# A written-out instruction order searched anew behind a common beginning: engines and PSUM banks of a long-convolution and MLP kernel

## The chip, the cores and the metric

The kernel runs on one core of one Trainium2 chip. The time is the device time of one execution in microseconds; a smaller one is better. The core has five engines that matter here, each with an instruction queue of its own that is worked off strictly in order: TensorE (PE, matmuls and weight loads, the latter shown as PEld), ScalarE (ACT), VectorE (DVE), GpSimd (POOL) and SyncE (SP, which issues nearly all DMAs). Engines wait for one another through semaphores. Matmul results land in PSUM, which has eight banks of 512 float32 values per partition; ACT or DVE must copy a result out ("evacuate" it) before PE may write that bank again.

## The reference

Two blocks, A and B, are applied twice to x of shape 1 x 2048 x 512, with the same k, v and weights each time:

```
def _A_ref(q, k, v, shift_k, ssm_k, ssm_D):
    ...                                   # k_shift: a causal filter of 4 taps along the sequence
    kv = k_shift * v
    ...
    y_f = kv_f * kf_f[None, :, :, :]      # FFT of kv times FFT of the 2048-tap filter ssm_k
    y = irfft2(y_f) ...                   # first 2048 positions, as bfloat16
    y = y + kv * ssm_D[None, None, :]
    return q * y
def _B_ref(x, w1, b1, w2, b2):
    y = _layernorm(x, axis=-1)
    h = _gelu(jnp.einsum("bsd,df->bsf", y, w1) + b1)          # 512 -> 1376
    return jnp.einsum("bsf,fd->bsd", h, w2) + b2              # 1376 -> 512
x = x + _A_ref(_layernorm(x), A_k, A_v, A_shift_k, A_ssm_k, A_ssm_D)
x = x + _B_ref(_layernorm(x), ...)
```

The last two lines stand twice. The convolution's y depends on k, v and the filter alone, so it is computed once and used in both layers.

## The kernel before, in words

**Two stages.** The first (up to about 83 us) computes y for all 2048 positions by a Fourier transform made of matmuls. The second runs two layers of norm, multiply by y, add, norm, and the MLP; in it all weights lie in SBUF.

**The first stage.** The 512 channels are worked in groups of 4 (128 groups). The steps, with the tags that the texts use: *ht*, the filter transposed (L528); *h1* and *h2*, the filter's two transform stages (L545, L558; 16 tiles each); *fir*, the four-tap filter of k and its product with v, on PE for channels 0 to 255 (L589, L606, L613) and on DVE for channels 256 to 511 (twelve products and sums of 128 x 2048 by L450 and two that multiply by v); *x1*, the first transform stage of kv (L545, 16 tiles); *x2*, its second stage (L651, 16 tiles), and behind each tile a product with the filter's transform on DVE (L450, 128 x 2048); *i1* and *i2*, the inverse transform's two stages (L674, 16 tiles; L731, 10 tiles). From x2 on the channels come in two parts, 0 to 255 and 256 to 511 (tags x2_0 and x2_64, and so on). Each tile of h1, h2, x1, x2 and i1 fills two PSUM banks, so four of them can be open at a time, and each is evacuated by one instruction of L453, on ACT or on DVE. Sixteen DMAs on SP copy the filter's transform to other partitions between h2 and the products (dma(dst, src) at the end of the h2 loop).

**The second stage.** The 2048 positions are 16 slices of 128. Layer 0 takes them in blocks of 1, 1, 2, 2, 2, 2, 2, 2, 2 slices, layer 1 in four blocks of 4. For each slice DVE computes a variance (L754, L756), POOL the inverse root (L760, L762), DVE the norm (L768), the product with y and the sum (L450), then a second variance and norm. The normed slice is transposed, by PE for slices 0 and 1 of layer 0 (L814, evacuated by L453), by a DMA on SP for all others (L807). Eleven tiles of the first MLP matmul per block (tag m1, L827) are each evacuated by a gelu on ACT (L832); the second MLP matmul takes a slice in three groups of 4, 4 and 3 steps (tag m2, L860), and DVE adds the result to x (L864). The last slice of layer 1 is cut into three column ranges (L849, L853). Output DMAs go out by pairs of slices.

**What sets the order.** Nothing is scheduled at run time. The code records 1114 operations, numbered in the order of recording, with what each reads and writes. Three written-out tuples of class Prog decide the rest: ORDER lists all operations, and each engine's queue is the part of ORDER that falls to it; SECOND lists the evacuations that go to the second of their two permitted engines (ACT first, DVE second); BANKS gives the first PSUM bank of each tile. arrange() reads them, and sync() works out the waits that they need: an operation waits for all earlier ones it depends on, and the first matmul of a tile waits for the evacuation of the tile that had its banks before.

```
        for at, i in enumerate(self.ORDER):
            o = self.ops[i]
            o.eng = o.engs[i in second]
            ...
            if tl is not None and tl.base is None:
                tl.base = self.BANKS[tl.i]
                for b in range(tl.base, tl.base + tl.nb):
                    if last[b] is not None:
                        for p in [p for p in last[b].ops if p.eng != PE] or last[b].ops[-1:]:
```

Of the kernel before, what the change touches and what calls it, by code (L numbers as in the profile page):

```python
# [38 lines left out]
class Prog:  # L39
# [3 lines left out]

    G = 4
    ORDER = (
# [43 lines left out]
    SECOND = (  # L89
        63, 64, 66, 67, 69, 72, 89, 97, 105, 127, 155, 161, 169, 175, 177, 215, 221, 239, 291, 349, 392)  # L90
    BANKS = (
# [7 lines left out]


    def __init__(self, nc):
        self.nc = nc
# [798 lines left out]
```

## Time and profile before

| | |
|---|---|
| median of 3 runs | 242.38 us (241.93 to 243.59) |
| span of the profiled execution, first to last instruction | 238.8 us |
| PE busy | 226.2 us (95%), 2312 matmul records |
| DVE busy | 171.6 us (72%) |
| ACT busy | 138.3 us (58%) |
| POOL busy | 41.3 us (17%) |
| granted TensorE clock | 1.000 |

The profiled execution's span is 3.6 us shorter than the median of the three runs; what lies around the span (start and end of the launch) makes the rest. The busy share of PE is no measure of its load, since matmul records overlap: a record of 379 ns can be followed by the next one some 220 ns later. The predictions' sums therefore use distances from start to start. An operation's number below is its number in ORDER; the trace has the instructions of each engine in that order, so each one's time can be read off.

### The profile page before, as it was taken

What the parts mean: (1) busy time and instruction counts of PE and PEld (TensorE: products, weight loads), DVE (VectorE), ACT (ScalarE), POOL (GpSimd) and SP (SyncE); (2) the same over time, 40 slices, a digit from 0 to 9 for tenths busy, and PEclk for the clock granted to TensorE, in tenths of its full rate; (3) what the DMA queues carried; (4) which work ended last, traced back from release to release, by engine and by line L of the source; (5) the groups of instructions that cost most, each with busy time, mean ns of one, the idle gap of its engine ahead of it and who ended that gap; (6) DMA issues with size and microseconds to landing.
All of it is one profiled execution on the core that took longest, in us unless ns stands there. A gap on an engine that the chain in (4) does not pass through costs nothing.

```text
span 238.8 us, 5555 instructions
## 1 busy us (share of the span) xinstructions
PE 226.2 (95%) x2312; PEld 151.6 (63%) x2332; DVE 171.6 (72%) x359; ACT 138.3 (58%) x225; POOL 41.3 (17%) x77
## 2 busy tenths in 40 slices
PE   7987989886999999999999999999999999999995
PEld 3875778875899886766766667644444444444543
DVE  0979999999999999999887999693793312030035
ACT  2598799999999995642754444342782042454100
POOL 2179000000013444041230310400220200000000
PEclk9999999999999999999999999999999999999999
DMA  6999949999960003111122022240013021310024
GB/s 241 364 342 383 383 148 253 249 272 309 379 227 0 3 0 68 26 23 31 37 47 44 0 48 44 45 88 3 0 22 66 3 44 31 101 44 3 0 71 148
DMA packets 37035, 27.40 MB, mean 115 GB/s; under 512 B 19506, under 2 KB 29969, under 8 KB 37010
## 3 DMA queue, kind: packets, MB, share of 16 engines
q1 hardware_dynamic: 36446, 26.91, 37.8%
q8 instruction: 18, 0.29, 0.5%
q10 hardware_dynamic: 564, 0.14, 0.4%
q14 instruction: 7, 0.06, 0.1%
HBM read 16.82 MB, written 2.10 MB: 79 GB/s over the span
## 4 chain that ended last, share of the span: by engine, by line
PE 77%; ACT 9%; DMA 4%; DVE 4%; SPq 3%; issue 3%; ACTq 0%
PE ps L860 31%; PE ps L827 30%; ACT ar L453 9%; PE ps L674 5%; PE ps L731 3%; SPq L439 3%; PE ps L545 3%; DMA ar<-in_A_ssm_k_dram 2%; DVE ar L453 2%; DMA ar<-ar 2%; PE ps L528 1%; PE ps L606 1%; PE ps L849 1%; DVE sm L754 1%; PE ps L589 1%
## 5 line engine op out<-in xcount | busy, mean ns | idle before, releaser
L832 ACT ACTIVATE ar<-ps,sm 128x256 bf16<-128x256 f32 (+4 forms) x143 | 64.7, 525 | 72.5 <-PE ps L827 68.1
L827 PE MATMUL ps<-ar 128*128 128x256 bf16 (+4 forms) x568 | 84.2, 297 | 0.2
L860 PE MATMUL ps<-ar 128*128 128x512 bf16 (+1 forms) x329 | 79.0, 379 | 0.6
L453 ACT ACTIVATE ar<-ps 128x1024 bf16<-128x1024 f32 (+1 forms) x81 | 72.5, 1057 | 9.0 <-PE ps L511 4.5
L827 PEld LDWEIGHTS ps<-ar 128*128 128x128 bf16 (+1 forms) x572 | 52.9, 100 | 29.8 <-ACT ar L832 0.5
L450 DVE TENSOR_TENSOR ar<-ar 128x512 bf16<-128x512 bf16 (+3 forms) x106 | 63.6, 634 | 2.0 <-DMA ar<-in_A_k_dram 1.3
L860 PEld LDWEIGHTS ps<-ar 128*128 128x128 bf16 (+1 forms) x341 | 33.1, 98 | 34.3 <-ACT ar L832 0.3
L864 DVE TENSOR_TENSOR ar<-ar,ps 128x512 bf16<-128x512 bf16 x31 | 20.6, 680 | 47.3 <-PE ps L860 47.3
L754 DVE BATCH_NORM_STATS2 sm<-ar 128x6 f32<-128x512 bf16 (+1 forms) x68 | 42.8, 647 | 0.1
L768 DVE TENSOR_SCALAR ar<-ar,sm 128x512 bf16<-128x512 bf16 x64 | 25.0, 407 | 7.8 <-POOL sm L762 5.2
L760 POOL TENSOR_SCALAR sm<-sm 128x2 f32<-128x2 f32 (+2 forms) x26 | 6.0, 232 | 93.9 <-DVE sm L756 93.3
L762 POOL TENSOR_TENSOR sm<-sm 128x2 f32<-128x2 f32 (+2 forms) x26 | 21.6, 832 | 2.2
L545 PE MATMUL ps<-ar 128*64 128x128 bf16 x512 | 17.1, 221 | 1.4 <-issue 0.8
L545 PEld LDWEIGHTS ps<-ar 128*64 128x64 bf16 x512 | 14.9, 110 | 3.2 <-issue 1.0
L674 PE MATMUL ps<-ar 128*128 128x128 bf16 x256 | 15.0, 220 | 0.6 <-ACT ar L453 0.6
L674 PEld LDWEIGHTS ps<-ar 128*128 128x128 bf16 x256 | 14.7, 114 | 0.8 <-ACT ar L453 0.8
L453 DVE CAST ar<-ps 128x1024 bf16<-128x1024 f32 x11 | 13.0, 1212 | 0.3 <-PE ps L558 0.3
L651 PE MATMUL ps<-ar 128*128 128x64 bf16 x256 | 9.8, 194 | 3.2 <-ACT ar L453 2.7
L453 DVE COPY ar<-ps 128x2048 bf16<-128x2048 bf16 (+1 forms) x8 | 8.2, 1024 | 6.4 <-PE ps L528 6.3
L651 PEld LDWEIGHTS ps<-ar 128*128 128x128 bf16 x256 | 8.2, 98 | 4.7 <-ACT ar L453 3.9
L756 DVE BATCH_NORM_AGGREGATE sm<-sm 128x2 f32<-128x6 f32 (+1 forms) x64 | 9.9, 171 | 0.3
L558 PE MATMUL ps<-ar 128*128 128x128 bf16 x128 | 8.6, 220 | 0.8 <-ACT ar L453 0.8
(34 smaller groups left out, 78.1 us busy)
## 6 DMA issues: line engine op xcount, KB each, us to landing
ar<-tab_s SPq DMA_DIRECT2D x16, 256.0 KB, 9.6
ar<-ar SPq DMA_DIRECT2D x16, 256.0 KB, 4.2
ar<-in_A_ssm_k_dram SPq DMA_DIRECT2D x4, 512.0 KB, 5.3
ar<-in_A_k_dram SPq DMA_DIRECT2D x8, 256.0 KB, 7.6
ar<-in_A_v_dram SPq DMA_DIRECT2D x8, 256.0 KB, 9.6
ar<-in_A_q_dram SPq DMA_DIRECT2D x4, 512.0 KB, 7.9
out_dram<-ar SPq DMA_DIRECT2D x7, 256.0 KB, 2.1
ar<-in_B_w_dram SPq DMA_DIRECT2D x1, 1376.0 KB, 12.6
```

The source lines that it names most:

```text
L450: return P.op(eng, lambda e: e.tensor_tensor(o, a, b, op), reads=[a, b] + list(more), writes=[o])
L453: f = {ACT: lambda e: e.activation(dst, src(), AF.Copy), DVE: lambda e: e.tensor_copy(dst, src())}
L545: r = e.matmul(Q(tl, 64 * ri, 64, i * 128, [1, 128]), w, m, start=True, stop=True)
L651: r = e.matmul(Q(tl, 0, 128, i * pitch, [1, n]), w, m, start=True, stop=True)
L674: r = e.matmul(Q(tl, 0, 128, i * 128, [1, 128]), w, m, start=q == 0, stop=q == 1)
L754: P.op(DVE, lambda e, sj=sj, x=x: e.bn_stats(sj, x), reads=[x], writes=[sj])
L762: P.op(POOL, lambda e: e.tensor_tensor(r, v, hf, ALU.pow), reads=[v, hf], writes=[r])
L768: P.op(DVE, lambda e: e.tensor_scalar(o, x, m, r, ALU.subtract, ALU.mult), reads=[x, m, r], writes=[o])
L827: r = e.matmul(Q(tl, 0, rows, 0, [1, w]), a, m, start=dk == 0, stop=dk == 3)
L832: P.op(ACT, lambda e, dst=dst, tl=tl, rows=rows, bias=bias, w=w: e.activation(dst, Q(tl, 0, rows, 0, [1, w]), AF.Gelu_apprx_tanh, bias=bia ...
L860: r = e.matmul(Q(tl, 0, 128, 0, [1, 512]), ins[fc][0], ins[fc][1], start=fc == 0, stop=fc == 10)
L864: P.op(DVE, lambda e, x=x, tl=tl: e.tensor_tensor(x, x, Q(tl, 0, 128, 0, [1, 512]), ALU.add), reads=[x], writes=[x], tile=tl)
```

## The change

ORDER, SECOND and BANKS get other values; nothing else differs but one blank line. The recorded operations, their sizes and their dependencies are the same 1114. Each engine's queue keeps its beginning: PE's first 31 operations (up to the first filter matmuls of channel block 0, started at 27.6 us), ACT's first 22 (up to the second h2 evacuation, 26.2 us), DVE's first 23 (to 31.7 us), SP's first 40. Behind that the queues hold the same work in another order. Thirteen evacuations change engine: h2 127, x1 161, 175 and 177, x2 215 and i1 239 go from DVE to ACT; h2 137, x1 163, 165 and 213, x2 218, i1 249 and i2 314 go from ACT to DVE. So DVE has 20 of the L453 evacuations of the transform's and transposes' tiles where it had 19. The first lines of the change, and SECOND, which shows the engines:

```
     ORDER = (
-        49, 0, 47, 8, 7, 1, 3, 6, 48, 14, 71, 68, 5, 72, 18, 17, 15, 12, 4, 69, 9, 70, 50, 16, 65, 13, 19, 94, 2, 53, 73, 96, 51, 52, 11,
...
+        49, 8, 0, 47, 1, 7, 48, 9, 6, 3, 4, 2, 14, 5, 18, 17, 15, 71, 12, 16, 13, 72, 68, 19, 11, 50, 69, 305, 65, 51, 28, 10, 52, 70, 73,
...
     SECOND = (
-        63, 64, 66, 67, 69, 72, 89, 97, 105, 127, 155, 161, 169, 175, 177, 215, 221, 239, 291, 349, 392)
+        63, 64, 66, 67, 69, 72, 89, 97, 105, 137, 155, 163, 165, 169, 213, 218, 221, 249, 291, 314, 349, 392)
     BANKS = (
...
```

The queues that result, where they differ most (numbers of matmuls in a row on PE, from the h2 stage on):

```
before: ... x1 160, x2 64, x1 64, x2 160, i1 64, x2 32, i1 112, i2 4, i1 80, i2 52, transposes 4, i2 8, m1 4, transposes 4, m1 44, m2 4, ...
after:  ... x1 144, x2 16, x1 32, x2 32, x1 16, x2 16, x1 48, x2 144, i1 32, x2 16, i1 32, x2 32, i1 192, i2 56, transposes 4, i2 8, m1 4, transposes 4, m1 72, m2 4, ...
before, last: ... m2 20, last slice 11, m2 45, last slice 22
after, last:  ... m2 69, last slice 33
```

On DVE an evacuation (213) stands between the products of x2's first part; before, one variance of layer 0 (376) stood between those of its second part. On SP the sixteen copies of the filter's transform stand as 4, 11 and 1 with the loads of q earlier and the load of W1 last.

More of the change, by code (lines that the diff above doesn't have):

```diff
@@ L45 @@
     ORDER = (
[43 rows of a table removed]
[43 rows of a table added]
     SECOND = (
-        63, 64, 66, 67, 69, 72, 89, 97, 105, 127, 155, 161, 169, 175, 177, 215, 221, 239, 291, 349, 392)
+        63, 64, 66, 67, 69, 72, 89, 97, 105, 137, 155, 163, 165, 169, 213, 218, 221, 249, 291, 314, 349, 392)
     BANKS = (
[7 rows of a table removed]
[7 rows of a table added]
     def __init__(self, nc):
```

100 rows, old and new, of tables (BANKS, ORDER) are left out of this document.

## The prediction

> **What bounds the kernel.** I read the page first: its busy line and the slices show PE at 9 from a third of the span on, DVE and ACT at 9 before that.
>
> ```profile
> PE 226.2 (95%) x2312; PEld 151.6 (63%) x2332; DVE 171.6 (72%) x359; ACT 138.3 (58%) x225; POOL 41.3 (17%) x77
> ...
> PE   7987989886999999999999999999999999999995
> PEld 3875778875899886766766667644444444444543
> DVE  0979999999999999999887999693793312030035
> ACT  2598799999999995642754444342782042454100
> ```
>
> So there are two regimes, and the windows table says where the border lies (columns: length, then busy time with instructions of PE, PEld, DVE, ACT and POOL, clock, DMA share, GB/s).
>
> ```profile
> 50.00:60.00 10.00, 7.33 (x186) 6.06 (x181) 10.00 (x10) 10.00 (x13) 0.00 (x0) 1.00 0.97 294
> 60.00:70.00 10.00, 9.45 (x179) 9.21 (x177) 10.00 (x11) 10.00 (x12) 0.52 (x1) 1.00 0.95 349
> ...
> 100.00:110.00 10.00, 9.95 (x63) 6.00 (x63) 9.96 (x29) 4.68 (x13) 3.83 (x8) 1.00 0.15 30
> ...
> 200.00:210.00 10.00, 9.95 (x48) 4.50 (x47) 1.61 (x3) 3.21 (x6) 0.00 (x0) 1.00 0.21 66
> ```
>
> Up to about 65 us ACT and DVE have no idle time and PE waits; afterwards PE has none. How full PE is there I take from the chain of work, whose pieces give the distance from matmul to matmul.
>
> ```profile
> 59.08 5.80 ACT ar L453 x6
> 64.92 6.56 PE ps L674 x112
> 71.49 0.44 PE ps L731 x4
> 71.92 4.47 PE ps L674 x80
> 76.39 5.68 PE ps L731 x52
> ...
> 83.76 2.57 PE ps L827 x44
> ...
> 203.89 4.32 PE ps L827 x20
> ...
> 224.86 9.68 PE ps L860 x44
> ```
>
> A 128-column matmul comes every 58 ns, one of 256 every 109, one of 512 every 216 (4.32/20). The first m1 matmul starts at 83.08 and the last matmul ends at 236.37, 153.3 us later. The work between: 341 of L860 and 176 of L827 at 216 ns (111.7), 308 at 109 (33.6), 88 at 57 (5.0), the last slice's 33 (2.4) and some transposes (0.3), together 153.0. **PE has no idle time worth naming after 83 us, and nothing in the change makes this work smaller.** The tail behind the last matmul is 2.4 us (one addition, one output DMA).
>
> Before 83 us PE does lose time. From 24.67 (first h2 tile) to 59.42 (first i1 tile) its groups at their own distances add up to 26.1 us in a stretch of 34.7: 8.6 us of waiting. From 59.42 to 83.08 it loses 0.8.
>
> **The change, stage by stage.** Durations are spacings in the timeline:
>
> ```profile
> 25.32 5.61 ACT L453 ACTIVATE ar<-ps 128x1024 bf16<-128x1024 f32 x6 [2.58 <-PE ps L558]
> 26.02 3.48 DVE L450 TENSOR_TENSOR ar<-ar 128x2048 bf16<-128x2048 bf16 x3
> ```
>
> Six evacuations in 5.61 us, one alone 1.02: 0.91 us each on ACT. Likewise 1.13 us for each 128 x 2048 instruction of DVE, and 1.13 for an evacuation on DVE.
>
> *To 25 us*: same queues, 0.
>
> *25 us to the first i1 tile of the second part* (before: 284 at 68.59). What ends last is the last product, since i1_64 reads all of them. DVE's queue from 173 (24.87 us) to that product holds, before, 27 of L450, four of L613, six evacuations and one variance (0.60); after, the same without the variance. Before: 42.8 us of work and 0.5 of waiting for PE (ahead of 127, at 40.20), the last product ending at 68.21. After: 42.2 of work. It waits too: evacuation 137 needs PE tile 136, fourth-last of h2; followed by hand through PE's and ACT's slots, 136 ends at 38.9 where DVE is free at 38.5, 0.5 us. Near the end product 271 is free 0.3 us ahead of ACT's evacuation 270. So 67.9 to 68.1, a gain of 0.1 to 0.3. PE reaches 292, the first i1_64 tile, when ACT has emptied the banks of 250: ACT's 49 evacuations from 121 to the last of i1_0 are as many as before, with 0.3 us of waiting in both (197 behind x1_2, which needs the DVE filter's last product). I get 292 at 68.4 against 68.59: **-0.2**, and for what my hand-followed waits may miss in some 45 alternations, -0.6 to +0.6.
>
> The copies on SP lie in this stretch. The long batch starts when h2 is done, at about 40.3 (before 41.5), and holds 11 copies where it had 9:
>
> ```profile
> 41.46 7.91 SPq L439 DMA_DIRECT2D ar<-ar x9
> ```
>
> 0.88 us each, and 4.2 (median) to landing. The four that product 231 needs are done with the eighth, 40.3 + 7.1 + 4.2 = 51.6; DVE comes there at 54.0. Product 256 needs the eleventh (54.2, DVE at 58.6), 274 the sixteenth, behind three loads (about 60, DVE at 63.1). Cover 2.4 to 4.4 us: cost 0. If it went, DVE, which has no idle time here, would pass the delay on in full. W1, now the last load, has until 83 us; before, SP's last load was issued at 59.2. The bias loads and POOL's copies of them stand earlier and wait for nothing that is late.
>
> *i1_64 to the first m1*: eight i1 tiles (0.92 each), ten i2 tiles (6.99) and four transposes (0.23) are 14.55 us of PE; before took 14.49 from 284 to 83.08, so PE alone bounds it. After: the same list, 68.4 + 14.55 = **82.95**, if nothing else comes late. What can: the norm of slice 0 (347), on which the transposes 348 wait. It follows i2 evacuation 324 (ACT, after PE tile 323 ends at 78.1, so to 78.8), then two products, two sums and a variance on DVE (with other work between, 1.3 us), 1.0 on POOL, the norm: 81.7. PE is there at 81.9. Cover 0.2 us, thin. Evacuation 314, now on DVE, waits for PE tile 313 at 76.3, with DVE ready at 75.7; all else on DVE stands behind it, and that 0.6 is in my count.
>
> *Second stage*: the same PE work, so the question is whether PE gets a wait. I set PE's running sum from 82.95 against DVE's. The late ones are the transposes of blocks 2 and 3: last norm ends at 89.6 and 92.9, SP issues two transposes of 1.3 us one behind the other, landing 2.5 after the issue: 92.2 and 95.7; PE comes at 92.9 and 96.4. Cover 0.7 each. Before had no more: block 3's second transpose was issued at 95.00 and PE took it at 97.52 without a wait. From block 4 on the cover is 1.3 to 3.5 us. DVE is 96% busy there, and I counted 3 us of waits for POOL in by 119 us; before has 4.1 from 83 to 175. Banks: of the tiles that are written again within 1.3 us of the matmul that their evacuation needs (3 for DVE's), before has 36 and after 18; the tightest stands at 0.71, and before went without a wait at 0.51. So **0**, bounded by 0 and +1.5 (both covers missed by half a microsecond or more).
>
> *Tail*: the last output goes through SP instead of ACT's queue, 32 KB landing in 1.5 or 1.6 us: 0.
>
> **Sum**: 238.8 - 0.2 = 238.6 us of span. The median lies 3.6 above the profiled span, and so I say 242.2 us against 242.38, **no change that can be told**; on this kernel about 1% (2.4 us) is what a measurement tells surely from none.
>
> A rule speaks against my floor: the Trainium skill (Perfetto Trace Analysis, Identifying the Most-Contended Engine) calls matmul busy time a bad metric and the share of LDWEIGHTS a good one. By it the PEld row, 63% here and 45% at 200 to 210 us, leaves PE room, and an order could take much more than 0.2 us. The same skill's TensorE: Matmul & The Clock Gate gives 215.7 ns from start to start for 512 columns; the trace has 216 and agrees. I hold to the spacings.
>
> **Rivals.** *Nothing moves* (0.66): as above, 241.4 to 243.2.
>
> *PE room* (0.03): PE's spacing could be shortened by better mixing of wide and narrow matmuls, hiding weight loads (98 ns) behind the wide ones. For: PEld at 45%. Against: 216 ns for 512 columns in long runs and in short ones alike (pieces of x3 and x44). If weight loads cost the 128-column ones 10 ns each, the 344 of i1 and m1 give -3.4 us: 238.8.
>
> *The front shortens by more* (0.08): i1's first tile is ready at 58.7 instead of 59.4, and if PE's 0.8 us of waiting up to 83 goes as well, -1.0 to -1.5: 241.
>
> *The thin covers fail* (0.11): the norm of slice 0 or the transposes of blocks 2 and 3 come late by half a microsecond each: +0.5 to +1.5, 243.4.
>
> *Slower, by one mechanism* (0.12): DVE falls behind between 41 and 66 us because ACT and DVE alternate as suppliers of PE. In the after queue x1_0's 163 and 165 are on DVE between filter products, and x2 cannot start before 165 (44.9). If PE's tiles reach DVE 0.6 us late at each of the five evacuations that it has there, the last product ends 3 us later, and as PE is full from there on, all of it is in the time: 245.2. It decides from the point where DVE idles at all between 41 and 66 us; before did not.
>
> That the change has no effect because PE's work is fixed is the first case. Chances: faster by over 1%: 0.03; within 1%: 0.85; slower by over 1%: 0.12. The range takes in the front's gain and the thin covers, and up to part of the last rival: 241.0 to 244.4.
>
> **What the profile after will show.** Last x2 product ending at 67.9 to 68.1; first i1_64 matmul near 68.4; first m1 near 83.0; then PE pieces that add up to 153.3 without a wait over 0.2 us; span 238.6. Wrong if DVE shows idle time between 41 and 66 us, if PE waits on DVE or a DMA before L814 or L827, or if W1 lands after 83 us.

## The result, and the profile after

The changed kernel takes **244.82 us** (median of 8 executions, 243.09 to 247.13), the kernel before, run beside it, 241.7 us. The ratio is 1.0111, with a 95% interval of 1.0083 to 1.0139: **slower by about 1.1%**. That lies above the forecast of 242.2 us and above its range. (The ratios in this document compare fast executions alone, of the changed kernel seven of the eight, so they needn't equal the quotient of the medians.)

In every execution the time is the span and 1.8 us (245.71 and 243.9 in the profiled one). The profiled execution of before, with its span of 238.8, was therefore one of about 240.6, below all eight that were timed (the lowest is 241.25).

The page of the changed kernel: the busy line, and the slices of PE, DVE, ACT and the granted clock. Line numbers are one lower than before (L826 is the first MLP matmul, L859 the second, L831 the gelu, L806 the transposes).

```profile
PE 229.0 (94%) x2313; PEld 153.8 (63%) x2332; DVE 177.3 (73%) x360; ACT 137.5 (56%) x224; POOL 41.5 (17%) x77
...
PE   7996999887899999799999999999999999999996
...
DVE  0889599999999999988997987975778652020233
ACT  2488399999999993482355182253363333347000
...
PEclk9999799999999999999999999999999999999999
```

Two slices of PE stand out: a 6 in the fourth slice (18 to 24 us) and a 7 in the seventeenth (98 to 104 us). The second one is inside the stage that I had called full. The list of PE's waits behind 84 us, of the kernel before (first fence, an empty list under its heading) and of the changed kernel in two profiled executions; the columns are the sum, the number and the longest, in us:

```profile
core 0 of [0], span 238.8 us
engine line waited for: us in total, times, longest us
```

```profile
PE ps L826 <- ACT ar L831: 1.6, 1, 1.6
PE ps L826 <- issue: 0.2, 1, 0.2
PE ps L826 <- DMA ar<-ar: 0.2, 1, 0.2
```

```profile
PE ps L826 <- DMA ar<-ar: 2.1, 1, 2.1
PE ps L826 <- ACT ar L831: 1.3, 1, 1.3
```

All of them are waits of a block's first m1 tile for its transposed slices. Where the list names the gelu on ACT, the tile waits for several semaphores, and the transpose is the last of them: in the first profile block 3's tile (operation 499) starts at 101.22, the second transpose of the block (496) landed at 101.13. Measured against the usual distances from matmul to matmul, PE waits 2.09 us behind the first m1 tile in the first profile and 3.62 in the second, where in the profile of before it waited for nothing (-0.02).

The chain of work between 84 and 150 us shows what has changed. Before, it runs over PE alone; in the changed kernel (second profile) over DVE, POOL and the transposes:

```profile
by line: PE ps L827 54.4%; PE ps L860 43.9%; ACT ar L832 1.3%; issue 0.7%
```

```profile
by line: DVE sm L753 28.7%; DVE ar L449 15.9%; DVE ar L767 13.5%; POOL sm L761 10.6%; DVE ar L863 8.0%; DMA ar<-ar 6.2%; DVE sm L755 5.7%; issue 4.1%; POOL sm L759 3.0%; ACT ar L452 2.9%; PE ps L826 1.6%; PE ps L859 0.7%; ACT ar L831 0.4%; 
...
144.57 4.09 DMA ar<-ar
148.71 1.05 PE ps L826 x8
```

The last two lines are the end of that chain: one transpose (758, block 8) that lands 4.09 us after its issue, and the m1 tile that waits for it. In the first profile the same transpose took 2.40:

```profile
146.68 2.40 DMA ar<-ar
149.12 1.05 PE ps L826 x8
```

**The front.** In the first profile the first h2 evacuation starts at 28.20 us instead of 25.32, although nothing of the queues up to there has changed. The rows of 20 to 30 us (columns as in the prediction) show a lower granted clock there, first the changed kernel, then the kernel before:

```profile
20.00:30.00 10.00, 7.39 (x94) 5.75 (x90) 7.43 (x8) 5.06 (x6) 4.50 (x4) 0.83 1.05 382
```

```profile
20.00:30.00 10.00, 8.27 (x114) 6.85 (x116) 9.67 (x9) 7.42 (x9) 3.79 (x2) 1.00 1.05 382
```

This belongs to the execution, not to the order: the second profile of the changed kernel has its first h2 evacuation at 26.10, and two of the experiments below, which have PE's front of the kernel before, have theirs at 27.16 and 27.17. From the first h2 evacuation to the first m1 tile it is 57.88 us in both profiles of the changed kernel and 57.76 before. So the stretch that I had worked out at most length takes the same time, and the loss is behind 84 us.

### The profile page after: what moved, and what is told of

Read it like the earlier page. It is cut to its first block, busy times and chain, and to the rows that moved or that the text cites. A ratio compares the mean times of both kernels' runs of the same rounds, so it can differ in the third digit from the quotient of the medians.

```text
span 243.9 us, 5564 instructions
## 1 busy us (share of the span) xinstructions
PE 229.0 (94%) x2313; PEld 153.8 (63%) x2332; DVE 177.3 (73%) x360; ACT 137.5 (56%) x224; POOL 41.5 (17%) x77
## 4 chain that ended last, share of the span: by engine, by line
PE 49%; DVE 20%; ACT 17%; POOL 8%; issue 4%; DMA 1%; POOLq 0%; DVEq 0%
PE ps L859 19%; PE ps L826 18%; ACT ar L452 17%; DVE sm L753 8%; PE ps L673 5%; DVE ar L449 4%; DVE ar L767 4%; POOL ar L519 4%; POOL sm L761 3%; PE ps L527 2%; DVE ar L863 2%; DVE sm L755 2%; PE ps L498 1%; PE ps L605 1%; PE ps L848 1%
## 5 line engine op out<-in xcount | busy, mean ns | idle before, releaser
L831 ACT ACTIVATE ar<-ps,sm 128x256 bf16<-128x256 f32 (+4 forms) x143 | 64.4, 529 | 74.3 <-PE ps L826 74.0
L826 PE MATMUL ps<-ar 128*128 128x256 bf16 (+5 forms) x568 | 82.2, 296 | 2.1 <-ACT ar L831 1.6
L859 PE MATMUL ps<-ar 128*128 128x512 bf16 (+1 forms) x330 | 77.5, 379 | 0.6
L826 PEld LDWEIGHTS ps<-ar 128*128 128x128 bf16 (+1 forms) x572 | 53.2, 100 | 30.5 <-ACT ar L831 1.8
L449 DVE TENSOR_TENSOR ar<-ar 128x512 bf16<-128x512 bf16 (+3 forms) x106 | 64.5, 635 | 1.8 <-DMA ar<-in_A_k_dram 0.6
L859 PEld LDWEIGHTS ps<-ar 128*128 128x128 bf16 (+1 forms) x341 | 33.1, 98 | 35.9 <-ACT ar L831 0.6
L753 DVE BATCH_NORM_STATS2 sm<-ar 128x6 f32<-128x512 bf16 (+1 forms) x68 | 43.4, 651 | 0.7
L767 DVE TENSOR_SCALAR ar<-ar,sm 128x512 bf16<-128x512 bf16 x64 | 24.5, 402 | 11.7 <-POOL sm L761 11.7
L673 PE MATMUL ps<-ar 128*128 128x128 bf16 x256 | 15.0, 220 | 0.9 <-DVE ar L449 0.5
L452 DVE CAST ar<-ps 128x1024 bf16<-128x1024 f32 (+1 forms) x12 | 14.0, 1171 | 0.2 <-PE ps L557 0.2
L755 DVE BATCH_NORM_AGGREGATE sm<-sm 128x2 f32<-128x6 f32 (+1 forms) x64 | 10.7, 175 | 1.0
L519 POOL TENSOR_SCALAR ar<-ar,sm 128x128 bf16<-128x128 bf16 x8 | 9.3, 1157 | 0.8
```

Of the source, the lines that this page charges most:

```text
L449: return P.op(eng, lambda e: e.tensor_tensor(o, a, b, op), reads=[a, b] + list(more), writes=[o])
L452: f = {ACT: lambda e: e.activation(dst, src(), AF.Copy), DVE: lambda e: e.tensor_copy(dst, src())}
L519: P.op(POOL, lambda e, o=o, t=t: e.tensor_scalar(o, IDN, t, None, ALU.mult), reads=[IDN, t], writes=[o])
L673: r = e.matmul(Q(tl, 0, 128, i * 128, [1, 128]), w, m, start=q == 0, stop=q == 1)
L753: P.op(DVE, lambda e, sj=sj, x=x: e.bn_stats(sj, x), reads=[x], writes=[sj])
L767: P.op(DVE, lambda e: e.tensor_scalar(o, x, m, r, ALU.subtract, ALU.mult), reads=[x, m, r], writes=[o])
```

## The experiments

Two theories. **O**: the new order of DVE's queue makes norms, and with them the transposes, late for PE. **L**: the 16 KB loads of PE's own instructions (18 in a run, DMA queue 8, kind "instruction") meet the transposes and make them land late. The rival of both: the front. In the texts written ahead of the runs, Theory 1 is O and L together and Theory 2 the front; Theory A is L and Theory B is O. Numbers are operation numbers; "waits" are PE's waits behind the first m1 tile in the profiled execution, summed from the distances in the trace as above. The texts written ahead of the runs speak of 36 and of two matmuls more; as issued they are 32 and none, and the table says so.

| kernel | waits, us | median, us | ratio to before, 95% interval |
|---|---|---|---|
| changed kernel, again | 3.62 | 244.87 | 1.0118 (1.0072 to 1.0164) |
| its front, second stage of before | 1.45 | 243.09 | 1.0068 (1.0040 to 1.0095) |
| front of before, its second stage | 4.12 | 245.36 | 1.0136 (1.0097 to 1.0175) |
| three variances later | 6.61, of which 5.06 ahead of blocks 3, 4 and 8 | 246.98 | 1.0175 (1.0121 to 1.0228) |
| changed, 32 matmuls more | 2.10 | 243.52 | 1.0092 (1.0059 to 1.0126) |
| before, unaltered (2 matmuls meant) | 0.64 | 241.23 | 0.9979 (0.9946 to 1.0011) |
| before, 32 matmuls more | -0.01 | 241.28 | 0.9996 (0.9957 to 1.0035) |
| before, taps earlier | 0.63 | 241.51 | 0.9974 (0.9940 to 1.0008) |
| changed, eight norms ahead | 1.30 | 242.58 | 1.0051 (1.0023 to 1.0079) |
| eight norms, 32 matmuls | 1.20 | 242.57 | 1.0039 (1.0005 to 1.0074) |
| eight norms, three variances | 1.63 | 242.90 | 1.0030 (1.0001 to 1.0060) |
| before, a norm made late | 1.52 | 243.24 | 1.0056 (1.0027 to 1.0085) |

The kernel before took 241.58, 241.63 and 241.85 us beside the first, second and third four of these rows.

### The changed kernel again

No edit.

> The changed kernel, unaltered, profiled a second time. In its first profile two places are late: the filter's first h2 evacuation at 28.20 us (before 25.32; the queues up to there are the same), and PE's wait of 1.75 us ahead of the first m1 tile of block 3 (operation 499), whose second transpose (496) landed at 101.13 because the first (498) took 2.33 us to issue while a 16 KB load of PE's instructions was under way at 96.12. Theory 1 (thin cover in the second stage): the wait of 1.5 to 2.1 us stands in this profile too, with the 2.3 us issue; the late h2 does not have to. Theory 2 (the loss is in the front, by what chance does at the start): the wait at block 3 is under 0.5 us here, and the time follows the first h2 evacuation. Median 244 to 245 us, ratio 1.008 to 1.014 by both.

Measured: 244.87 us. The wait at block 3 is there again (1.51 us), with the slow issue of the first transpose (2.03 us, landing 3.14 after its start), and the late h2 is not. A wait of 2.23 at block 8 comes in, which was 0.31 in the first profile. So Theory 1 holds and Theory 2 falls. The executions at full clock of the changed kernel lie in two heaps, 243.1 to 243.5 and 244.6 to 245.4; that block 8's wait, which is there or not, makes the two is likely but only argued, since two profiles show it.

### Each half alone

```
front of the changed kernel  = PE up to 391, ACT to its last i2 evacuation (318), DVE up to 392, POOL up to 389, SP up to 302
front of the kernel before   = PE up to 391, ACT to its last i2 evacuation (328), DVE up to 392, POOL up to 389, SP up to 301
behind it: all other operations in the order of the other kernel
```

> Front of the changed kernel (up to the last transposes of slice 1, the last h2-to-i2 evacuations and their DVE work), then the queues of the kernel before for the second stage. Nothing is left out. Theory 1: no wait of PE behind the first m1 tile, ratio 0.997 to 1.003. Theory 2 or a slower front order: ratio 1.007 to 1.014, as the changed kernel itself.

> The other half alone: front of the kernel before, second stage of the changed one. Theory 1: PE waits 1.5 to 2.1 us ahead of block 3's first m1 tile and 0.3 us each ahead of blocks 8 and 10, ratio 1.006 to 1.010. A slower front order as the cause: ratio 0.997 to 1.003.

Measured: 1.0068 for the changed front, against the forecast of Theory 1, and 1.0136 for the changed second stage, more than the forecast. The trace tells why the first is not 1.000: PE waits 1.0 us ahead of tile 368 in block 1 (the list names the gelu on ACT, 0.8 us), and 0.55 us ahead of block 2 (453), whose transpose had 0.27 us to spare in the kernel before. The likely reason, argued only, is the seam: the second stage of before is timed against its own front. The other half has about 1 us of such waits ahead of block 3 too, and then 0.17 (block 3), 0.76 (block 4) and 2.20 us (block 8). So the halves don't add up to the whole, but in each the excess time (1.5 and 3.8 us) is about the sum of PE's waits behind 84 us (1.45 and 4.12).

### Three variances behind block 3's second norm

```
 DVE of the changed kernel
-... 488, 581, 484, 445, 485, ... 530, 532, 497, 583, 582, 495, 538, 584 ...
+... 488, 484, 445, 485, ... 530, 532, 497, 495, 581, 583, 582, 538, 584 ...
```

> The changed kernel with three variance operations of blocks 5 (581, 583, 582; 0.69, 0.69 and 0.16 us on DVE) moved behind block 3's second norm (495), so that block 3's norms end about 0.7 and 1.4 us earlier; all else as in the changed kernel. Theory 1: the wait at 499 falls from 1.75 to between 0 and 0.95 us (0.95 if the first transpose still takes 2.3 us to issue), the time falls by 0.8 to 1.75 us: ratio 1.001 to 1.008 where the changed kernel has 1.011. Theory 2 or the front: no change, ratio 1.008 to 1.014.

Measured: 1.0175, above the changed kernel's 1.0111, though the two intervals overlap. In the profiled execution the granted clock was at half from 150.6 to 154.0 us, which makes most of the other 1.6 us of the 6.61. At its place the edit did what Theory 1 said: the wait at 499 fell from 1.51 to 0.69. But PE came earlier to the next blocks and found their transposes later: 1.98 us at block 4, 2.37 at block 8. There two transposes landed 4.17 and 4.46 us after their issue; in both a load of PE's instructions had started 1.95 us after it. This set the two theories O and L against each other.

### Moving the loads: 32 matmuls more

Each x2 tile issues its first matmul again, which writes the same values. That changes no queue's order, but PE's instruction loads come some 250 instructions apart, so all later ones move.

```
-                for i, w, m in ins:
+                for i, w, m in ins[:1] * (2 + (k0 < 32)) + ins:
```

(With `(k0 == 0)` in place of the bracket: the run meant to have two matmuls more.)

Both edits do less than the texts below say. `f` runs when the queues are written out, after the loop over `k0` has ended, and reads the last value, 112. So `k0 < 32` and `k0 == 0` are false in every tile: the first edit adds two matmuls to each of 16 tiles, 32 in all, and the second adds none. The traces agree: this line has 256 weight loads in the kernel before, 288 with the first edit and 256 with the second. **The run with two matmuls is the kernel before, unaltered, a second time.**

> The changed kernel with 36 matmuls more: in each x2 tile the first matmul is issued two times more (four of the tiles: three times more), writing the same values. That is about 2.1 us more of PE work (36 x 58 ns), in a stretch where PE waits. It moves every later 16 KB load of PE's instructions, which come every 256 instructions of PE, ahead by 72 instructions, that is 4 to 8 us. By the positions in the two profiles of the changed kernel no load then falls between the issue and the landing of a transpose of blocks 2 to 8, save one at the start of a transpose of block 6. Theory A (the loads, colliding with the transposes, make them late): PE waits under 0.5 us in all behind the first m1 tile where the changed kernel waits 2.1 and 3.6, every transpose lands within 2.4 to 2.6 us of its issue, and the time falls by 1.5 to 3.5 us although work was added: ratio 0.998 to 1.005 against the kernel before. Theory B (thin cover alone: DVE's norms come too late in the new order): waits stay at 1.5 to 3.6, time as the changed kernel or up to 2 us longer, ratio 1.010 to 1.020.

> The kernel before with the same 36 matmuls more: the control for what they cost themselves. The loads then lie clear of the transposes, save at the very start of two with covers of 2.3 and 1.4 us. Theory A: no wait in the second stage, and what is measured is the cost of the 36 in the front: 0 to 1 us, ratio 0.999 to 1.005. If 36 of them cost more than 2.4 us here, the run with the changed kernel has to be read against that.

> The kernel before with two matmuls more, one in the first x2 tile of each part (0.1 us of PE work, where it waits). It moves the later instruction loads ahead by four instructions, 0.3 to 0.5 us at blocks 2 and 4: the load near the second transpose of block 2 (446) then starts some 1.85 us after its issue and that near the second of block 4 (548) some 2.0, where it was 2.28 and 2.31. Theory A: loads that start 1.85 to 2.0 us after the issue made the landing 1.5 to 2.0 us later in three profiles, and the kernel before has covers of 0.3 and 0.05 us there, so PE gets waits of 1.2 to 2 us at block 4 and perhaps as much at block 2; ratio 1.005 to 1.014. Theory B: two matmuls in the shadow change nothing, ratio 0.998 to 1.002.

Measured, in the changed kernel: block 3's first transpose lands again as it should, and its wait is gone. The DMA view of the stretch in which it is issued, with its 16 KB load (the kernel with eight norms ahead, where this transpose is the same) and without (32 matmuls more):

```profile
q8 instruction: 1, 0.02, 6.9%
issues: line engine op xcount, KB each, median us to landing
ar<-ar SPq DMA_TRANSPOSE x1, 3.1
```

```profile
DMA packets 0, 0.00 MB, mean 0 GB/s; under 512 B 0, under 2 KB 0, under 8 KB 0
## 3 DMA queue, kind: packets, MB, share of 16 engines
issues: line engine op xcount, KB each, median us to landing
ar<-ar SPq DMA_TRANSPOSE x1, 2.4
```

The median fell from 244.8 to 243.5 although work was added, less than Theory A's forecast (0.998 to 1.005), and the intervals of the two ratios overlap. What stayed are waits behind transposes that landed within 2.4 to 2.7 us of their issue: 0.61 us at block 4, 0.34 at block 6, 0.93 at block 8, 0.37 at block 10. So L is not all of it; these are O's, but for 0.3 us of the 0.61, where the landing took 2.68 us instead of 2.4.

In the kernel before, the same 32 cost nothing (0.9996), though three transposes of blocks 6 and 8 now landed 3.6 to 4.2 us after their issue, as the loads had moved onto them. They had 1.4 to 2.3 us to spare, and 0.7 and 1.8 were left. This is the view at the issue of the first transpose of block 8 (758), before and with the 32:

```profile
ar<-ar SPq DMA_TRANSPOSE x1, 2.4
```

```profile
ar<-ar SPq DMA_TRANSPOSE x1, 4.2
```

The run with two matmuls tests neither theory, as it adds none. What it shows is how much the kernel before differs from itself: a ratio of 0.9979, whose interval takes in 1, and another place for a load. The load at block 2 stayed where it was (2.27 us behind the issue, 2.28 before), the one at block 4 came 3.7 us earlier (22.3 us behind the first m1 tile, 26.0 before), slowed the issue of that block's first transpose to 1.85 us and gave a wait of 0.66 us. The place of a load is thus not fixed to the instruction. In the run of the next section PE's queue is that of the kernel before too, and the same load came at 22.3 us, with a wait of 0.64 at block 4. What else sets it stays open.

### The start: tap matrices earlier on POOL

```
 POOL of the kernel before
-53, 67, 64, 44, 45, 56, 59, 57, 60, 310, 54, 61, 58, 55
+53, 56, 59, 67, 57, 60, 64, 44, 45, 61, 58, 54, 55, 310
```

> The kernel before with POOL's first operations in another order: the diagonal tap matrices that the first filter tile needs stand ahead of the two small additions (64, 67) and two memsets, so that they end near 17 us instead of 22.6. It tests whether the start (up to the filter's first h2 evacuation, 25.3 us before, 26.1 and 28.2 in the changed kernel's profiles) hangs on POOL. If it does: first h2 evacuation earlier by 0.3 to 1 us and the time with it, ratio 0.996 to 0.999. If PE's own chain to 154 (end 23.09) sets it: no change, ratio 0.999 to 1.001.

Measured: 0.9974, no difference that the interval tells, nor does it decide between the two forecasts; the unaltered kernel before gave 0.9979 in the last section. The trace says more. The tap matrix 58 started at 14.86 us instead of 19.96, but PE's tile 154, which stands ahead of the fir tile that needs it (172), has its second matmul at 22.27 us, 22.08 before. Tile 172 went on at 24.06 (23.15 before), at half the granted clock from 22.54 us on. So in this profile POOL doesn't set the start.

### DVE's order alone

```
 DVE of the changed kernel
-549, 686, 688, 589, 691, 547        +549, 547, 686, 688, 589, 691
-697, 472, 793, 746, 869, 698, 651, 653
+697, 651, 653, 472, 793, 746, 869, 698
-876, 817, 807, 885, 886, 804, 755, 815, 949, 950, 757
+876, 755, 757, 817, 807, 885, 886, 804, 815, 949, 950
-903, 732, 684, 955, 905, 956, 959, 968, 962, 963, 960, 901
+903, 905, 901, 732, 684, 955, 956, 959, 968, 962, 963, 960
```

> The changed kernel with eight norms of DVE moved ahead in its queue (547 of block 4 behind 549; 651 and 653 of block 6 behind 697; 755 and 757 of block 8 behind 876; 905 and 901 of block 10 behind 903); block 3, PE, ACT, POOL and SP as in the changed kernel. In the run with 36 more matmuls the transposes of these blocks landed within 2.7 us of their issue and PE still waited for them, 0.61, 0.34, 0.93 and 0.37 us (net 2.1 us), since DVE did other work ahead of the norms. Theory O (DVE's order makes the norms late, the loads of PE's instructions add to it): the waits at blocks 4, 6, 8 and 10 go, 1.5 us at block 3 stays (load behind the first transpose); the time falls by 1 to 2.3 us against the changed kernel: ratio 1.002 to 1.008. Theory L (the loads alone): moved norms meet loads as before; no change, ratio 1.008 to 1.014.

> Both together: the eight norms ahead, and the 36 repeated matmuls in the x2 tiles, which keep the loads of PE's instructions off the transposes of block 3. Theory O: no wait of PE over 0.3 us behind the first m1 tile, the whole loss is back: ratio 0.997 to 1.003. If 1.005 or more remains, something else than these waits costs time in the changed kernel, and the front would be the place.

> The eight norms ahead, and for block 3 the three variance operations (581, 583, 582) behind its second norm (495), without the 36 matmuls. The three variances alone brought block 3's wait from 1.5 to 0.7 us, but the waits at blocks 4 and 8 grew to 2.0 and 2.4, by loads that met the transposes. Theory O: with norms early enough a late landing is covered, so waits sum to 0.5 to 1.5 us, ratio 1.001 to 1.006. Theory L: 1.010 or more.

Measured: 242.58 us, ratio 1.0051; its interval ends below that of the changed kernel (1.0079 against 1.0083). **Eight moved norms, and nothing else, take the excess of the median from 3.1 to 0.7 us, that of the ratio from 1.1 to 0.5%.** The waits at blocks 4, 6, 8 and 10 are gone, the 1.4 at block 3, which the edit doesn't touch, is what is left, and the chain of 84 to 150 us runs over PE again (the ACT in both views is that wait, whose transpose landed last):

```profile
PE ps L827 <- ACT ar L832: 1.3, 1, 1.3
```

```profile
by line: PE ps L827 53.3%; PE ps L860 44.5%; ACT ar L832 1.8%; PE ps L814 0.3%; issue 0.1%
```

With the 32 matmuls as well, block 3's wait is gone, but block 4 gets one of 0.94: this time an instruction load of 8 KB on DMA queue 14 came 1.9 us behind the issue of 548, which landed 3.43 us after it. With the three variances, block 3 is on time, a load meets block 2's transposes (0.16), and 548 again lands late (1.10); another 0.41 at 99.5 us is a wait of a tile of block 2 (465), for which the list names DVE's addition L864. Both forecasts of no or nearly no loss are half met: 1.0039 and 1.0030, each with some 1.2 to 1.6 us of waits that moved but didn't go.

### The kernel before, with one norm made late

```
 DVE of the kernel before
-497, 536, 495, 590, 539, 537, 591, 375, 540, 739, 587, 642, 541
+497, 536, 539, 537, 375, 540, 541, 495, 590, 591, 739, 587, 642
```

> The kernel before with five operations of DVE (539, 537, 375, 540, 541; 2.6 us in all) moved ahead of block 3's second norm (495); no load of PE's instructions lies there (the nearest start at 92.0 and 109.0 us, the transpose at 95.0). The kernel before has 0.09 us of cover at this place. Theory O: the transpose lands about 2.2 us later, PE waits 1.8 to 2.2 us ahead of block 3, and all of it is in the time: ratio 1.006 to 1.010, the other blocks unchanged or with more cover. If PE's later tiles make it up again: ratio under 1.004.

Measured: 1.0056, a median of 1.4 us more. PE waits 1.54 us ahead of block 3 (the list names ACT, as in the changed kernel; the transpose landed at 101.22, the tile starts at 101.31), with both transposes landing in the usual 2.4 us. So the order of DVE alone, with no load near, costs its wait in full:

```profile
PE ps L827 <- ACT ar L832: 1.4, 1, 1.4
```

## Why the prediction was wrong

**The step that failed** is the second stage: "cover 0.7 each" for blocks 2 and 3, "1.3 to 3.5 us" from block 4 on, and "So 0, bounded by 0 and +1.5". The time between the landing of a block's last transpose and PE's arrival, from the traces (a negative number is a wait):

| block | 2 | 3 | 4 | 5 | 6 | 7 | 8 |
|---|---|---|---|---|---|---|---|
| before | 0.27 | 0.09 | 0.05 | 0.91 | 2.31 | 2.25 | 1.41 |
| before, second profile (unaltered run) | 0.28 | 0.09 | -0.61 | 1.56 | 2.31 | 2.27 | 1.42 |
| changed, second profile | 0.29 | -1.42 | 0.45 | 1.75 | 0.47 | 3.68 | -2.19 |
| changed, 32 matmuls more | 0.29 | 0.15 | -0.56 | 1.01 | -0.25 | 3.68 | -0.89 |
| changed, eight norms ahead | 0.29 | -1.34 | 0.16 | 1.68 | 1.92 | 3.68 | 1.52 |

Two terms of it were wrong.

- *DVE's running sum.* The row with 32 matmuls more, where no transpose of blocks 2 to 8 landed later than 2.7 us after its issue, shows the order by itself: cover is half a microsecond short of my 0.7 at blocks 2 and 3, and below zero at 4, 6 and 8, where I had at least 1.3. PE's side of the sum held: it would have been at block 3 13.4 us behind the first m1 tile, as forecast (96.4 - 82.95). DVE's side was short: the last norms of blocks 2 and 3 end 7.07 and 10.46 us behind that tile, in both profiles of the changed kernel, where I had 6.65 and 9.95. Which entry of the sum was short isn't known. Up to 119 us it was not the waits for POOL's inverse roots: I had counted 3 us, both profiles have 1.7. Behind that they grow: between 84 and 150 us the changed kernel has 4.3 and 5.5 us in the two profiles, the kernel before 0.7.

```profile
DVE ar L768 <- POOL sm L762: 0.7, 3, 0.3
```

```profile
DVE ar L767 <- POOL sm L761: 5.5, 7, 1.2
```

  These waits don't decide it, though: the kernel with eight norms ahead still has 4.6 us of it and hardly a loss. What counts is which work stands ahead of a norm that a transpose, and behind it PE, waits for. At block 8 the changed order has five operations of layer 1 between the norms' last input on DVE and the first norm, and eight ahead of the second.
- *The landing at 2.5 us.* I took it from two transposes as if it were a constant. It is 2.4 to 2.6 as long as no instruction load falls in; when one starts 0.45 to 2.0 us behind the issue it is 3.1 to 4.5, up to 2 us late, where I had covers of 0.7 at blocks 2 and 3.

Both work together. In the second profile the 1.5 us at block 3 are late landings by themselves (with 2.4 us, the second transpose would have landed 0.15 us ahead of PE), and my cover of 0.7 would have left 0.9 of them; at block 8, 1.7 of 2.2 us are the late landing and the rest is the order. How much of the whole loss is due to each of the two isn't a fixed share, since a wait at one block gives the transposes of later blocks more time.

**The base.** "The median lies 3.6 above the profiled span": 1.8 of that is the launch, the other 1.8 is that this execution was shorter than the median. Against the 241.7 us of eight executions my forecast was no change or 0.5 us more. Counted from 241.7, the forecast gain of 0.2 us makes 241.5, and the miss is only larger.

**What held.** From the first h2 evacuation on, the front came out as worked out: first i1_64 tile 43.25 us behind it (43.1 forecast), the last x2 product's end 42.83 (42.6 to 42.8), first m1 tile 57.88 (57.6; before 57.76). So the gain of 0.2 us isn't there, and no loss either. The copies of the filter's transform landed 2.5, 4.0 and 4.3 us ahead of products 231, 256 and 274 (2.4 to 4.4 forecast) in the second profile, W1 landed at 73.1, ahead of 83. The last matmuls and the tail took what they took before.

**The rivals.** *The thin covers fail* (0.11) was the mechanism, at the wrong size: I had priced it at 0.5 to 1.5 us by two covers missed by half a microsecond, and it was 2.1 and 3.6 us in the two profiles, since blocks 4, 6, 8 and 10 were thin as well and since a landing can be late by 2 us. *Slower by DVE falling behind between 41 and 66 us* (0.12) had the right sign and engine but the wrong place: DVE is busy 24.97 of 25 us there. *PE room* (0.03) got no support: nothing ran faster than the kernel before.

One of the marks that I had named as "wrong if" stood in the result, PE waiting on a DMA before L827, and one sign that I had forecast didn't: no wait over 0.2 us behind the first m1 tile.

## What to carry to other kernels

An order that is tuned to a few tenths of a microsecond has its whole value in the waits that it avoids, and a list of covers must be worked out for every hand-over to the bounding engine, with what stands ahead of the supplier in its own queue; one total of busy time says nothing of it. A transfer's time to landing is not a constant: read its spread from all transfers of its kind in the trace, and give a hand-over the cover of a late one. To see which engine bounds a stage, ask for the chain of that stage alone: here it went from PE to DVE and back, while the busy shares moved by a few per cent. The chain names the engine, not the size: it follows the last wait of the stretch, and a wait of 0.32 us at block 8 in the first profile turns it to DVE as 2.23 us do in the second. And see in the trace that an edit is there: the number of weight loads told that one of the runs above had no edit at all.

## What the runs showed of the hardware

**Loads of instructions delay DMA transposes.** In the 14 profiled executions there are 252 transposes of blocks 2 to 8 of layer 0 and the first of layer 1. For 184 of them no load of instructions (16 KB on queue 8, 8 KB on queue 14) overlaps the time from issue to landing, and all of these landed 2.40 to 2.56 us after the start of their issue. By where a load starts (six of the fourth row, whose load comes after the landing, are among the 184):

| load | starts after the transpose's issue, us | transposes | landing after the issue, us |
|---|---|---|---|
| PE's, 16 KB | 0.45 to 0.59 | 6 | 3.05 to 3.83 (issue itself 1.9 to 2.3 instead of 1.2 to 1.3) |
| PE's, 16 KB | 0.84 to 1.10 | 3 | 3.62 to 4.07 |
| PE's, 16 KB | 1.85 to 2.00 | 7 | 3.97 to 4.46 |
| PE's, 16 KB, no other load near | 2.27 to 2.95 | 14 | 2.40 to 2.50 |
| queue 14's, 8 KB, no load of PE near | 1.74 to 1.94 | 9 | 3.05 to 3.43 |

The remaining ones landed within 2.4 to 3.0 us, and two, with loads of both kinds near, at 3.6. Queue 8 moves 18 loads of 16 KB, 63 bytes for each of PE's 4,699 instructions in the trace of the kernel before. Queue 14 moves seven of 8 KB, more than ACT, with 240 instructions, can need at that size; whose they are the trace doesn't tell.

The runs with 32 matmuls more moved the loads by changing nothing but PE's count of instructions, and the late landings moved with them; so this is more than a coincidence in time. The Trainium skill (Runtime: NRT & Kernel Launch, Instruction fetch mechanics) says that the sequencer refills instructions in blocks of 16 KiB, 256 instructions, by a DMA queue of its own, and that the cost of crossing a block is mostly hidden. The blocks agree with the 18 loads of 16 KB here, which stand 203 to 288 instructions of PE apart in the second stage, some 250 on average. The lists of PE's waits there have none over 0.2 us without a named cause, so PE itself hardly waits for its loads; here the cost came out at a third place, a transpose on SP's queue that another wait hung on.

**The clock.** In four of the profiled executions, with either front, the granted clock fell to half for one stretch of 3.41 us: at 22.5 to 28.0 us in three, whose first h2 evacuation came at 27.2 to 28.2 us instead of 25.3 to 26.1, and at 150.6 us in the run with three variances later. These are the stretch at half clock and the equally long one ahead of it in the kernel before with one norm made late, then two such stretches of the changed kernel's second profile, where the clock stayed full:

```profile
19.22:22.63 3.41, 1.84 (x42) 1.42 (x41) 3.41 (x4) 3.40 (x5) 3.22 (x3) 1.00 1.05 383
22.63:26.04 3.41, 3.41 (x22) 2.23 (x20) 2.37 (x2) 0.39 (x1) 1.58 (x2) 0.50 1.06 382
```

```profile
21.04:24.46 3.42, 1.83 (x27) 1.44 (x23) 3.42 (x4) 2.47 (x3) 3.30 (x2) 1.00 1.05 379
24.46:27.87 3.41, 3.19 (x47) 2.73 (x46) 2.89 (x3) 1.77 (x2) 0.00 (x0) 1.00 1.05 383
```

Ahead of the four drops PE was busy for 1.20, 1.20, 1.81 and 1.84 us of 3.41, and between 7 us and the last matmul only two other such stretches of the 14 profiles have as little, 1.83 and 1.85 us; these were followed by the full clock. So an idle PE goes with the drop, but at 1.8 us doesn't decide it by itself. At 150.6 us the idle time was the wait of 2.37 us at block 8: there one long wait was followed by another 1.7 us at half clock. Nothing here was run to test it.

No kernel of this study was measurably faster than the kernel before; of those with the changed order the nearest by ratio, eight norms ahead and three variances later, is still 0.3% slower. By their medians (242.58, 242.57 and 242.90 us) the three kernels with eight norms ahead can't be told apart.
